# Single-bank PSUM tiles, VectorE alone for two-operand work, and the leaky gate in one ScalarE instruction, in the Strassen part of an attention and two-layer feed-forward kernel

## The chip, the core and the metric

The kernel runs on one core of one Trainium2 chip. The metric is device time in microseconds. TensorE (PE in the profile) multiplies matrices into PSUM, which has 8 banks of 512 fp32 columns in each of 128 partitions; VectorE (DVE), ScalarE (ACT) and GpSimd (POOL) do the element-wise work; SyncE (SP) issues the DMAs. In this kernel GpSimd touches SBUF tiles only.

## What is computed

A windowed attention makes a matrix `x` of 3072 tokens by 512, and two feed-forward layers follow. Cut to what matters:

```python
x = moe(attention(q, k, v, mem_k, mem_v))      # layer 1: h = x @ w_in; g = h * clip(h + 3, 0, 6) / 6; g @ w_out
h = x @ w_in2                                  # layer 2, first product: 512 -> 2048
g = np.maximum(0.01 * h, h)                    # the leaky gate
out = g @ w_out2                               # layer 2, second product: 2048 -> 512
```

The precision of fp32 is kept by writing an operand as a high part (rounded to fp32r by a copy) and a low part (the operand minus its high part), and by three products in place of one: high by high, low by high, high by low.

## The kernel before

**Blocks.** The tokens are taken in six blocks of 512 columns, features on the partitions. A matmul is 128 by 128 by 512 columns. Layer 1 (`hidden`, `output`) makes for each of 16 slices `f` of the hidden 2048 features 12 matmuls of the first product, the gate, and 12 matmuls of the second product into four PSUM banks that stay open over all 16 slices.

**The Strassen part.** The first product of layer 2 is made for two blocks at a time (three phases, p = 0, 1, 2) by a Strassen scheme: a phase has 8 steps `i`, and a step makes seven products (`seven`, in the order 1, 6, 5, 7, then 2, 3, 4) of 6 matmuls each for two slices of hidden features of both blocks. Four PSUM banks b1, b2, b3, b5 take them: products 1, 6, 5 and 7 open b1, b2, b3 and b5, and their results are read out into an SBUF tile `ut`; products 2, 3 and 4 are then accumulated on top of b1, b3 and b5. So product 2 must wait until product 1's result has been read from b1, 3 until 5's has been read from b3, and 4 until 7's has been read from b5. In code order each product is three groups of two matmuls.

The results: for the first block of the pair (slices f1 and f2) the gate's output goes to `r` and is parted into the tile `g` (`two_parts`: a copy for the high part, a subtraction for the low part); for the second block it goes to `ys` and by DMA to the DRAM array `later`, and comes back (`again`) when that block's second product is made. Between the products of a step stand two slices (12 matmuls each) of the first block's second product (`output("2", 2p, f)`, called y below): one between product 7 and product 2, one after product 4. After the 8 steps come the last slices of the first block (13, 14, 15) and 15 of the 16 slices of the second block; the sixteenth stands inside the next phase's first step.

**Operands of a phase and a step.** `x_pair` makes, around the end of the phase before, the seven right-hand operands in two quarters (`x_quarter`): four loads from `spill`, four differences (`t_1`, `sub`) and seven partings (`parts_of`). `w_set` makes the left-hand operands one step ahead: two loads into `wm`, four sums or differences of 256 columns (`form`, L830) into `st`, and four partings (`two`).

**PSUM.** Two tiles `ya` and `yb` of two banks each, two tiles `h` of one bank, one tile `at` of two banks (attention, then a Strassen bank pair). `banks_of` hands a set of four banks to a phase or a block: either `h`, `h` and the two halves of `at`, or the halves of `ya` and `yb`. Phases 0 and 2 use the first set, phase 1 the second; the blocks' second products use the set that is free. Waits are put in by the tile framework, by tile: an instruction that writes a part of a tile waits for reads of that tile that stand earlier in the program, whichever half they read.

**What sets the order.** `schedule` runs the tasks in a simulated time with a cost per task, keys as priorities and a list of engines that may take each task (the first is preferred, the second taken if the first would be much later). All products are chained, so PE's order is fixed. Differences and low parts in the Strassen part name VectorE and GpSimd; high parts name ScalarE and VectorE. Each engine then works its own list strictly in that order.

**Names of lines in the trace of before.** L877 the Strassen matmuls, L684 the second products, L630 the first product of layer 1; L281 copies and high parts; L284 differences and low parts; L894 `plus` (sums from PSUM or SBUF); L905 `leak` (the gate on SBUF); L925 and L927 the gate of product 2 (a scaled copy on ScalarE, a maximum on VectorE); L715 and L717 copies of finished outputs.

Of the kernel before, what the change touches and what calls it, by code (L numbers as in the profile page):

```python
# [35 lines left out]
N = 512  # L36
# [169 lines left out]
def tile_attn_moe_moe2(ctx: ExitStack, tc: tile.TileContext, raw, w1i, w1o, w2i, w2o, out):  # L206
# [16 lines left out]
    for y in "ab":  # L223
        pools[f"y{y}"] = (ps_y, [128, 2, 512], F32)
# [439 lines left out]
    def output(lay, j, f, c0, n):
# [8 lines left out]
        ys = list(dict.fromkeys(b for b, _ in banks))  # L673
# [31 lines left out]
    def y_out(lay, j, f, t0, n, d, y, k, two):  # L705
# [16 lines left out]
        if two and f == KF - 1:  # L722
            l = add(lambda e: nc.sync.dma_start(out=make(s), in_=half[j, d]), {"SP": dma(n * 512)}, key - 8, after=[yhalf[j, d], *firsts], allocs=[s])
            k = add(plus, {"DVE": dve(n)}, key, after=[k, l], uses=[s, y[0]])
        else:
            k = add(take, {"DVE": dve(n)} if d % 2 else {"ACT": act(n, 50.0)}, key, after=[k], allocs=[s], uses=[y[0]])
# [22 lines left out]
    def x_quarter(p, j, key, need):  # L749
# [13 lines left out]
        def sub(out, x, y, after, allocs=(), uses=()):  # L763
            return add(lambda e: minus(e, out(), x(), y()), {"DVE": dve(N), "POOL": pool(N)}, key, after=after, allocs=allocs, uses=uses)

        def parts_of(name, of, own, after):
            bufs = xop[p, name]
            first = xtask[p, name][0][:1], xtask[p, name][1][:1]
            hi = add(lambda e: copy(e, operand(p, name, 0, j).bitcast(F32R), of()), {"ACT": act(N), "DVE": dve2(N)}, key, after=after + first[0], allocs=[] if first[0] else bufs[:1], uses=[own] + (bufs[:1] if first[0] else []))
            new = not first[1] and len(bufs) == 2  # L770
            lo = add(lambda e: minus(e, operand(p, name, 1, j).bitcast(F32R), of(), operand(p, name, 0, j).bitcast(F32)), {"POOL": pool(N), "DVE": dve(N)}, key, after=[hi] + first[1], allocs=bufs[1:] if new else [], uses=[own, bufs[0]] + ([] if new else bufs[1:]))
# [21 lines left out]
        t1 = add(t_1, {"DVE": dve(N), "POOL": pool(N)}, key, after=[got["b11"], got["b12"]], allocs=[tt], uses=[src["b11"], src["b12"]])  # L793
# [12 lines left out]
    def w_set(p, i, key):  # L806
# [19 lines left out]
        def form(out, x, y, op, after, allocs=(), uses=()):  # L826
# [4 lines left out]
            return add(fn, {"DVE": dve(256), "POOL": pool(256)}, key, after=after, allocs=allocs, uses=[*raws, *uses])  # L831
# [6 lines left out]
        def two(t, src, n, after):  # L838
# [8 lines left out]
            hi = add(fn_hi, {"ACT": act(n), "DVE": dve2(n)}, key + 0.5, after=after + gate, allocs=[ts[t]], uses=[src])  # L847
            lo = add(fn_lo, {"POOL": pool(n), "DVE": dve(n)}, key + 0.6, after=[hi], uses=[src, ts[t]])
# [7 lines left out]
    def seven(p, i, n):  # L856
# [14 lines left out]
        alloc = [to[0]] if fresh and n != 7 and not (n == 6 and to[1] is not None) else []  # L871
# [11 lines left out]
        us = [to[0], t, *xb]  # L883
# [6 lines left out]
        def plus(out, x, y, opts, after, allocs=(), uses=()):  # L890
            def fn(e):
                for q in allocs:
                    make(q, ([128, 2, N], F32) if q is ut else None)
                engine(e).tensor_tensor(out=out(), in0=x(), in1=y(), op=ALU.add)  # L894
            return add(fn, opts, key, after=after, allocs=allocs, uses=uses)

        def take(q, b, after, allocs=()):
            def fn(e):
                for x in allocs:
                    make(x, ([128, 2, N], F32))  # L900
                copy(e, ut.t[:, q], bank(b))
            return add(fn, {"ACT": act(N, 50.0), "DVE": dve(N)}, key, after=after, allocs=allocs, uses=[b[0]] + ([] if allocs else [ut]))
# [154 lines left out]
```

## Time and profile before

| | |
|---|---|
| median of 3 runs | 1195.41 us (1194.85 to 1195.47) |
| the profiled execution's own time | 1192.55 us |
| its span, first to last instruction | 1190.8 us |
| PE busy | 1111.6 us, 93% of the span |
| DVE, ACT, POOL busy | 53%, 40%, 33% |
| mean granted TensorE clock | 0.987 |
| matmuls in the chain that ended last | 83% of the span |

The chain that ended last is followed back from the last instruction, and is mostly PE. So the reading asks where PE stands still: the list of waits names for each engine who ended them, the timeline shows them one by one, and the starts in the chain give the length of a step to compare with its matmuls. The first 620 us are attention and layer 1; the Strassen part runs from 627.7 us to the end.

### The profile page before, as it was taken

Reading aid. Unit: us, or ns where it says so; the run is one execution under the profiler, and the core shown is the slowest. Engines: PE = TensorE matmul, PEld = TensorE weight load, DVE = VectorE, ACT = ScalarE, POOL = GpSimd, SP = SyncE. Lnnn points to the kernel's source line nnn. Section 1 sums busy time; section 2 is a strip of 40 time slices with the busy share of each in tenths; the row PEclk is TensorE's granted clock in tenths of the full one; section 3 lists DMA queues with packets and bytes.
Section 4 is the critical chain, followed back from the end, with each engine's and each line's share of the span. In section 5 each row is a group of like instructions: output and inputs, shape, how many; then the busy total and the mean of one; then the engine's idle time right before and its main releaser. Section 6 shows DMA issues by size and latency. Waiting matters only on the chain.

```text
span 1190.8 us, 19604 instructions
## 1 busy us (share of the span) xinstructions
PE 1111.6 (93%) x7632; PEld 897.2 (75%) x7632; DVE 625.4 (53%) x988; ACT 472.5 (40%) x1154; POOL 387.7 (33%) x319
## 2 busy tenths in 40 slices
PE   4599999999999999999999999899888899999998
PEld 3487888888888888888887777677666677777776
DVE  5789975554435535415517666744544571655310
ACT  4557655445554544433324333333222332322222
POOL 1030000011232232125524443664344474444343
PEclk9699999999999999999999999899999999999999
DMA  8894454654445534321103332622121260311150
GB/s 195 256 244 143 144 152 131 180 158 134 139 140 149 138 96 131 97 62 53 36 1 115 98 104 101 209 82 80 62 62 54 74 235 19 99 61 62 38 184 36
DMA packets 85341, 135.50 MB, mean 114 GB/s; under 512 B 8448, under 2 KB 41216, under 8 KB 85248
## 3 DMA queue, kind: packets, MB, share of 16 engines
q1 hardware_dynamic: 85248, 134.25, 37.3%
q8 instruction: 60, 0.98, 0.4%
q14 instruction: 33, 0.27, 0.1%
HBM read 98.57 MB, written 35.65 MB: 113 GB/s over the span
## 4 chain that ended last, share of the span: by engine, by line
PE 83%; DVE 5%; ACT 3%; DMA 3%; issue 3%; POOL 2%; SPq 2%; POOLq 0%; DVEq 0%; ACTq 0%
PE h L630 21%; PE ya L684 15%; PE yb L684 15%; PE at L877 7%; PE h L877 5%; PE h L684 5%; PE at L684 5%; PE yb L877 4%; PE ya L877 3%; ACT w L281 2%; PE at L506 1%; DMA w<-in_w1i 1%; DMA w<-in_raw 1%; PE at L445 1%; DVE ys L894 1%
## 5 line engine op out<-in xcount | busy, mean ns | idle before, releaser
L284 POOL TENSOR_TENSOR g<-r,g 128x512 fp32r<-128x512 f32 x108 | 143.2, 1326 | 463.3 <-ACT g L281 459.2
L684 PE MATMUL ya<-g,w 128*128 128x512 f32 x864 | 266.8, 394 | 4.8 <-ACT g L281 2.1
L684 PE MATMUL yb<-g,w 128*128 128x512 f32 x864 | 264.2, 391 | 0.0
L630 PE MATMUL h<-xh,w 128*128 128x512 f32 x768 | 195.5, 395 | 1.9 <-ACT xh L281 1.9
L684 PEld LDWEIGHTS ya<-g,w 128*128 128x128 f32 x864 | 160.8, 188 | 41.0 <-ACT g L281 3.5
L684 PEld LDWEIGHTS yb<-g,w 128*128 128x128 f32 x864 | 163.1, 189 | 34.8
L630 PEld LDWEIGHTS h<-xh,w 128*128 128x128 f32 x768 | 144.2, 190 | 33.1 <-ACT xh L281 3.1
L646 DVE SCALAR_TENSOR_TENSOR r<-r,h 128x512 f32<-128x512 f32 x96 | 65.9, 686 | 171.7 <-ACT r L643 171.6
L281 ACT CAST g<-r 128x512 fp32r<-128x512 f32 x144 | 89.7, 623 | 158.2 <-DVE r L646 51.4
L643 ACT ACTIVATE r<-h,three 128x512 f32<-128x512 f32 x96 | 66.6, 693 | 155.6 <-PE h L630 155.1
L630 PE MATMUL h<-xl,w 128*128 128x512 f32 x384 | 104.4, 394 | 0.6 <-issue 0.6
L684 PE MATMUL h<-g,w 128*128 128x512 f32 x288 | 89.8, 396 | 1.5 <-DVE g L284 1.0
L684 PE MATMUL at<-g,w 128*128 128x512 f32 x288 | 89.1, 394 | 0.0
L877 PE MATMUL at<-w 128*128 128x512 f32 x288 | 74.9, 398 | 14.9 <-DVE ys L894 9.4
L630 PEld LDWEIGHTS h<-xl,w 128*128 128x128 f32 x384 | 72.2, 189 | 16.2 <-issue 1.0
L284 POOL TENSOR_TENSOR g<-w,g 128x512 fp32r<-128x512 f32 x45 | 60.3, 1340 | 55.3 <-ACT g L281 55.3
L877 PEld LDWEIGHTS at<-w 128*128 128x128 f32 x288 | 52.5, 188 | 33.1 <-DVE ys L894 14.5
L684 PEld LDWEIGHTS h<-g,w 128*128 128x128 f32 x288 | 54.8, 191 | 14.6 <-DVE g L284 1.5
L281 ACT CAST g<-w 128x512 fp32r<-128x512 f32 x48 | 29.8, 621 | 85.9 <-PE at L684 55.8
L684 PEld LDWEIGHTS at<-g,w 128*128 128x128 f32 x288 | 54.9, 191 | 11.9
L284 DVE TENSOR_TENSOR w<-st,w 128x512 fp32r<-128x512 f32 x28 | 35.9, 1294 | 48.7 <-ACT w L281 48.7
L284 POOL TENSOR_TENSOR w<-wm,w 128x512 fp32r<-128x512 f32 (+1 forms) x44 | 54.8, 1250 | 8.6 <-ACT w L281 6.7
(163 smaller groups left out, 1502.0 us busy)
## 6 DMA issues: line engine op xcount, KB each, us to landing
wm<-w322i SPq DMA_DIRECT2D x48, 256.0 KB
later<-ys SPq DMA_DIRECT2D x48, 256.0 KB
w<-later SPq DMA_DIRECT2D x24, 512.0 KB
a<-in_raw SPq DMA_DIRECT2D x44, 224.0 KB
w<-in_w1i SPq DMA_DIRECT2D x16, 512.0 KB
w<-in_w1o SPq DMA_DIRECT2D x16, 512.0 KB
w<-in_w2i SPq DMA_DIRECT2D x16, 512.0 KB
w<-in_w2o SPq DMA_DIRECT2D x16, 512.0 KB
```

Source lines behind the costliest of these rows:

```text
L281: nc.scalar.copy(out, in_) if e == "ACT" else engine(e).tensor_copy(out=out, in_=in_)
L284: engine(e).tensor_tensor(out=out, in0=a, in1=b, op=ALU.subtract)
L445: nc.tensor.matmul(ps.t[h * CHUNK:(h + 1) * CHUNK, par, i * W:(i + 1) * W], qk[h // 2].t[r, gp, (h % 2) * G + c * CHUNK:(h % 2) * G + (c + ...
L506: nc.tensor.matmul(pv.t[(h % 2) * D:(h % 2 + 1) * D, par, (h // 2) * 2 * G + i * CHUNK:(h // 2) * 2 * G + (i + 1) * CHUNK], v[h // 2].t[r, ...
L630: nc.tensor.matmul(h.t[:, :n], w.t[:, 1 if p == 1 else 0, k * 128:(k + 1) * 128], x[:, k, c0:c0 + n], start=(p == 0 and k == 0), stop=(p = ...
L643: nc.scalar.activation(out=make(r)[:, :n], in_=h.t[:, :n], func=AF.Relu, bias=three[:, 0:1], scale=1.0)
L646: nc.vector.scalar_tensor_tensor(out=r.t[:, :n], in0=r.t[:, :n], scalar=6.0, in1=h.t[:, :n], op0=ALU.min, op1=ALU.mult)
L684: nc.tensor.matmul(bank(banks[d])[:, c0:c0 + n], w.t[:, 1 if p == 1 else 0, d * 128:(d + 1) * 128], g.t[:, 1 if p == 2 else 0, :n], start= ...
L877: nc.tensor.matmul(bank(to), t.t[:, 1 if q == 1 else 0, o, kt * 128:(kt + 1) * 128], operand(p, name, 1 if q == 2 else 0, kt).bitcast(F32R ...
L894: engine(e).tensor_tensor(out=out(), in0=x(), in1=y(), op=ALU.add)
```

## The change

It edits five things, in the Strassen part and in the PSUM tiles.

1. **PSUM.** `ya`, `yb` become four one-bank tiles `y`; `at` is kept for attention and is then replaced by two one-bank tiles `hx`. The first four units of attention use two-bank tiles `ab`, `ac`, closed when the first `y` is made. A bank is now a tile, so `seven` and `output` name single tiles.
2. **Engines.** Every difference, sum and low part of `x_quarter`, `w_set`, `seven` and `again` names VectorE alone; the high parts in `x_quarter` and `w_set` name ScalarE alone. Layer 1 keeps GpSimd for its low parts.
3. **The leaky gate.** `leak` and the two instructions for product 2 become one ScalarE activation, Prelu with slope 0.01.
4. **Product 5.** It is no longer copied to `ut`; VectorE adds it to the sum of 1 and 6 at once.
5. **Product 7.** Its bank is added to that sum straight into `ys`; the extra sum over SBUF (on GpSimd or VectorE) is gone.

```diff
-    for y in "ab":
-        pools[f"y{y}"] = (ps_y, [128, 2, 512], F32)
+    for a in "bc":
+        pools[f"a{a}"] = (ps_b, [128, 2, 512], F32)
...
-    places |= {"ya": 1, "yb": 1, "h": 2, "at": 1}
+    places |= {"ab": 1, "ac": 1, "y": 4, "h": 2, "at": 1, "hx": 2}
...
+        if b.tag in ("hx", "y") and b.tag not in pools:
+
+            (attention if b.tag == "hx" else begin).close()
+            pools[b.tag] = (ctx.enter_context(tc.tile_pool(name=b.tag, bufs=places[b.tag], space=PSUM, side="right" if b.tag == "hx" else "left")), [128, 512], F32)
...
     def banks_of(other):
-        if other:
-            t = Buf("at")
-            return [(Buf("h"), None), (Buf("h"), None), (t, 0), (t, 1)]
-        a, b = Buf("ya"), Buf("yb")
-        return [(a, 0), (a, 1), (b, 0), (b, 1)]
+        return [Buf(t) for t in (("h", "h", "hx", "hx") if other else "yyyy")]
...
         def sub(out, x, y, after, allocs=(), uses=()):
-            return add(lambda e: minus(e, out(), x(), y()), {"DVE": dve(N), "POOL": pool(N)}, key, after=after, allocs=allocs, uses=uses)
+            return add(lambda e: minus(e, out(), x(), y()), {"DVE": dve(N)}, key, after=after, allocs=allocs, uses=uses)
...
-            return add(fn, {"DVE": dve(256), "POOL": pool(256)}, key, after=after, allocs=allocs, uses=[*raws, *uses])
+            return add(fn, {"DVE": dve(256)}, key, after=after, allocs=allocs, uses=[*raws, *uses])
...
-            hi = add(fn_hi, {"ACT": act(n), "DVE": dve2(n)}, key + 0.5, after=after + gate, allocs=[ts[t]], uses=[src])
-            lo = add(fn_lo, {"POOL": pool(n), "DVE": dve(n)}, key + 0.6, after=[hi], uses=[src, ts[t]])
+            hi = add(fn_hi, {"ACT": act(n)}, key + 0.5, after=after + gate, allocs=[ts[t]], uses=[src])
+            lo = add(fn_lo, {"DVE": dve(n)}, key + 0.6, after=[hi], uses=[src, ts[t]])
...
         def leak(r, after):
-            return add(lambda e: nc.vector.scalar_tensor_tensor(out=r.t, in0=r.t, scalar=0.01, in1=r.t, op0=ALU.mult, op1=ALU.max), {"DVE": dve(N)}, key, after=[after], uses=[r])
+            return add(lambda e: nc.scalar.activation(out=r.t, in_=r.t, func=AF.Prelu, alpha=0.01), {"ACT": act(N)}, key, after=[after], uses=[r])
...
-        low = {"POOL": pool(N), "DVE": dve(N)}
-        dv = {"DVE": dve(N)}
+        low = {"DVE": dve(N)}
...
         elif n == 5:
-            done[5] = take(1, b3, [k, done[1]])
+            done[5] = plus(lambda: ut.t[:, 1], lambda: bank(b3), lambda: ut.t[:, 0], [k, done[6]], uses=[ut, b3])
         elif n == 7:
-            done[7] = plus(lambda: ut.t[:, 1], lambda: bank(b5), lambda: ut.t[:, 1], dv, [k, done[5]], uses=[ut, b5[0]])
             r = Buf("ys")
-            q = plus(lambda: r.t, lambda: ut.t[:, 0], lambda: ut.t[:, 1], {"POOL": pool(N), **dv}, [done[7], done[6]], allocs=[r], uses=[ut])
-            put(r, f2, leak(r, q))
+            done[7] = plus(lambda: r.t, lambda: bank(b5), lambda: ut.t[:, 1], [k, done[5]], allocs=[r], uses=[ut, b5])
+            put(r, f2, leak(r, done[7]))
         elif n == 2:
             r = Buf("r")
-            q = add(lambda e: nc.scalar.mul(make(r), bank(b1), 0.01), {"ACT": act(N, 50.0)}, key, after=[k, *rs[-1:]], allocs=[r], uses=[b1[0]])
+            q = add(lambda e: nc.scalar.activation(out=make(r), in_=bank(b1), func=AF.Prelu, alpha=0.01), {"ACT": act(N, 50.0)}, key, after=[k, *rs[-1:]], allocs=[r], uses=[b1])
             rs.append(q)
-            q = add(lambda e: nc.vector.tensor_tensor(out=r.t, in0=bank(b1), in1=r.t, op=ALU.max), dv, key, after=[q], uses=[r, b1[0]])
             two_parts("2", a, f1, r, q, key, low)
...
-        two_parts("2", 2 * p + 1, f, r, k, key, {"POOL": pool(N), "DVE": dve(N)}, f % 2)
+        two_parts("2", 2 * p + 1, f, r, k, key, {"DVE": dve(N)}, f % 2)
```

PE's matmuls and transposes stand in the same order in both programs; what changes on PE is where it waits. First PE, in a step in the middle of phase 0, products 1, 6, 5 and 7 (`h` holds b1 and b2; `at`, later `hx`, holds b3 and b5); before:

```order
L877 MATMUL h<-xh,w 128x512 x2
L877 MATMUL h<-xh,w 128x512 [waits Pool_49]
L877 MATMUL h<-xh,w 128x512 x3
L877 MATMUL h<-xl,w 128x512 x2
L877 MATMUL h<-xl,w 128x512 [waits Pool_49]
L877 MATMUL h<-xl,w 128x512 x3
L877 MATMUL at<-w 128x512 [waits DVE_49]
L877 MATMUL at<-w 128x512 x7
L877 MATMUL at<-w 128x512 [waits Activation_49]
L877 MATMUL at<-w 128x512 x3
```

The same four products of the change, on PE:

```order
L877 MATMUL h<-xh,w 128x512 [waits Activation_49]
L877 MATMUL h<-xh,w 128x512 x5
L877 MATMUL h<-xl,w 128x512 [waits Activation_49]
L877 MATMUL h<-xl,w 128x512 x5
L877 MATMUL hx<-w 128x512 [waits DVE_49]
L877 MATMUL hx<-w 128x512 x5
L877 MATMUL hx<-w 128x512 [waits DVE_49]
L877 MATMUL hx<-w 128x512 x5
```

The wait in the middle of product 7 (the ninth matmul on `at`) is gone, and with it those in the middle of 1 and 6; every wait now stands at a product's start.

VectorE in one step of phase 0 (numbers tell buffers apart; L894 sums, L905 and L927 gate, L830 `form`, L284 low parts); before:

```order
L894 TENSOR_TENSOR w_7029<-h_7026,w_7029 128x512
L830 TENSOR_TENSOR st_7039<-wm_6985,st_7035 128x256
L284 TENSOR_TENSOR w_7059<-st_7039,w_7059 128x512
L894 TENSOR_TENSOR w_7029<-at_7043,w_7029 128x512
L905 SCALAR_TENSOR_TENSOR ys_7081<-ys_7081 128x512
L284 TENSOR_TENSOR w_7093<-wm_7061,w_7093 128x512
L927 TENSOR_TENSOR r_7100<-h_7016,r_7100 128x512
L284 TENSOR_TENSOR w_7104<-wm_7067,w_7104 128x512
L894 TENSOR_TENSOR ys_7118<-at_7043,w_7029 128x512
L905 SCALAR_TENSOR_TENSOR ys_7118<-ys_7118 128x512
L894 TENSOR_TENSOR r_7130<-at_7043,w_7029 128x512
L905 SCALAR_TENSOR_TENSOR r_7130<-r_7130 128x512
```

The same step of the change on VectorE, from product 6's sum on (L290 is what L284 was):

```order
L894 TENSOR_TENSOR w_7051<-h_7048,w_7051 128x512
L894 TENSOR_TENSOR w_7051<-hx_7057,w_7051 128x512
L830 TENSOR_TENSOR st_7075<-wm_7036 128x256
L830 TENSOR_TENSOR st_7079<-wm_7028,wm_7036 128x256
L830 TENSOR_TENSOR st_7075<-st_7075,wm_7028 128x256
L290 TENSOR_TENSOR w_7065<-wm_7028,w_7065 128x512
L830 TENSOR_TENSOR st_7079<-wm_7028,st_7075 128x256
L290 TENSOR_TENSOR w_7073<-wm_7036,w_7073 128x256
L290 TENSOR_TENSOR w_7087<-st_7075,w_7087 128x512
L290 TENSOR_TENSOR w_7095<-st_7079,w_7095 128x512
L894 TENSOR_TENSOR ys_7109<-hx_7067,w_7051 128x512
L290 TENSOR_TENSOR g_7125<-r_7118,g_7125 128x512
```

The gate's four instructions are gone from VectorE, and all four forms and four low parts of the next step's weights now stand between the sums of products 5 and 7 (rows one, two and eleven; row twelve is the low part of a `g`); after the last row the sums of products 3 and 4, two low parts of `w_out` slices and a second low part of `g` complete the step.

Last, VectorE at the change from phase 0 to phase 1, from product 3's sum in the last step on (the operands of phase 1 are made here: `a`, `xh`, `xl` and `w`); before:

```order
L894 TENSOR_TENSOR ys<-at,w 128x512
L284 TENSOR_TENSOR a<-a,w 128x512
L905 SCALAR_TENSOR_TENSOR ys<-ys 128x512
L894 TENSOR_TENSOR r<-at,w 128x512
L284 TENSOR_TENSOR xl<-w,xl 128x512
L905 SCALAR_TENSOR_TENSOR r<-r 128x512
L830 TENSOR_TENSOR st<-wm 128x256 x2
L830 TENSOR_TENSOR st<-st,wm 128x256
```

The same place on VectorE in the change:

```order
L894 TENSOR_TENSOR ys<-hx,w 128x512
L290 TENSOR_TENSOR g<-r,g 128x512
L894 TENSOR_TENSOR r<-hx,w 128x512
L290 TENSOR_TENSOR w<-a,w 128x512
L290 TENSOR_TENSOR a<-a,w 128x512
L290 TENSOR_TENSOR xl<-w,xl 128x512
L290 TENSOR_TENSOR xl<-a,xl 128x512
L290 TENSOR_TENSOR w<-a,w 128x512
L290 TENSOR_TENSOR g<-r,g 128x512
```

Both low parts of `g` (for slices 14 and 15 of block 0) and the low parts of the operands have come over from GpSimd's list, and five instructions now stand between product 4's sum (`r<-hx`) and the low part of slice 15.

## Rows read from the trace of the kernel before

**Rows 1.** The page, part 1: busy time, share of the span, instructions.

```profile
PE 1111.6 (93%) x7632; PEld 897.2 (75%) x7632; DVE 625.4 (53%) x988; ACT 472.5 (40%) x1154; POOL 387.7 (33%) x319
```

**Rows 2.** Stretch table of phase 1's steps: length, PE, PEld, DVE, ACT, POOL, clock, DMA.

```profile
813.10:942.10 129.00, 113.61 (x475) 87.16 (x474) 62.42 (x101) 32.47 (x59) 50.04 (x40) 1.00 0.23 74
```

**Rows 3.** PE's waits: who waited for whom, total us, times, longest.

```profile
PE at L877 <- ACT w L281: 10.9, 16, 0.8
PE at L877 <- DVE ys L894: 9.4, 12, 0.8
PE yb L877 <- DVE ys L894: 6.7, 7, 2.0
PE yb L877 <- ACT w L281: 5.4, 8, 0.7
PE ya L877 <- ACT w L281: 5.3, 7, 0.8
```

**Rows 4.** The chain that ended last: start, us, what.

```profile
595.04 2.72 PE h L630 x12
...
627.68 2.72 PE h L877 x12
...
813.07 2.72 PE ya L877 x12
...
844.29 1.83 PE ya L877 x8
...
862.39 1.83 PE ya L877 x8
...
1004.44 2.72 PE h L877 x12
```

**Rows 5.** Timeline, all engines, products 6, 5, 7: start, us, engine, line, what, [idle before].

```profile
709.22 1.52 PE L877 MATMUL h<-xl,w 128*128 128x512 f32 x6
709.42 0.59 ACT L281 COPY w<-h 128x512 f32<-128x512 f32 x1 [0.69 <-PE h L877]
...
712.60 0.59 ACT L281 COPY w<-at 128x512 f32<-128x512 f32 x1 [0.71 <-PE at L877]
...
713.23 0.97 PE L877 MATMUL at<-w 128*128 128x512 f32 x3 [0.68 <-ACT w L281]
```

**Rows 6.** Timeline, all engines, change from phase 0 to 1.

```profile
751.86 1.73 POOL L284 TENSOR_TENSOR w<-a,w 128x512 fp32r<-128x512 f32 x1
...
752.37 1.77 DVE L284 TENSOR_TENSOR w<-a 128x512 f32<-128x512 f32 x1
...
754.79 0.69 DVE L284 TENSOR_TENSOR a<-a 128x512 f32<-128x512 f32 x1
754.87 1.76 POOL L284 TENSOR_TENSOR xh<-w,xh 128x512 fp32r<-128x512 f32 x1 [1.28 <-ACT xh L281]
...
755.39 0.69 DVE L927 TENSOR_TENSOR r<-h,r 128x512 f32<-128x512 f32 x1
...
763.13 0.73 PE L684 MATMUL ya<-g,w 128*128 128x512 f32 x2 [1.77 <-ACT g L281]
...
764.94 2.07 PE L684 MATMUL ya<-g,w 128*128 128x512 f32 x4 [1.07 <-POOL g L284]
...
766.37 0.41 DVE L284 TENSOR_TENSOR w<-wm,w 128x256 fp32r<-128x256 f32 x1
```

**Rows 7.** Stretch table just after that wait, columns as in rows 2.

```profile
765.00:770.00 5.00, 5.00 (x12) 3.93 (x13) 4.73 (x9) 2.59 (x5) 1.33 (x1) 0.50 0.57 196
```

**Rows 8.** Timeline of ACT late in layer 1, where phase 0's operands are made.

```profile
591.35 0.62 ACT L281 CAST g<-r 128x512 fp32r<-128x512 f32 x1 [4.07 <-DVE r L646]
```

**Rows 9.** Timeline, all engines, the last matmuls and the last copies out.

```profile
1184.34 1.52 PE L684 MATMUL at<-g,w 128*128 128x512 f32 x6
...
1185.89 0.69 DVE L717 TENSOR_SCALAR ys<-at 128x512 f32<-128x512 f32 x1 [0.67 <-PE at L684]
1186.62 0.60 ACT L715 ACTIVATE ys<-at 128x512 f32<-128x512 f32 x1 [2.17 <-DVE ys L717]
```

More of the change, by code (lines that the diff above doesn't have):

```diff
@@ L672, in output @@
         banks = ybuf[lay, j]
-        ys = list(dict.fromkeys(b for b, _ in banks))
+        ys = banks
         g, w = gbuf[lay, j, f, c0], wbuf[lay + "o", f]
@@ L723, in y_out @@
             l = add(lambda e: nc.sync.dma_start(out=make(s), in_=half[j, d]), {"SP": dma(n * 512)}, key - 8, after=[yhalf[j, d], *firsts], allocs=[s])
-            k = add(plus, {"DVE": dve(n)}, key, after=[k, l], uses=[s, y[0]])
+            k = add(plus, {"DVE": dve(n)}, key, after=[k, l], uses=[s, y])
         else:
-            k = add(take, {"DVE": dve(n)} if d % 2 else {"ACT": act(n, 50.0)}, key, after=[k], allocs=[s], uses=[y[0]])
+            k = add(take, {"DVE": dve(n)} if d % 2 else {"ACT": act(n, 50.0)}, key, after=[k], allocs=[s], uses=[y])
         k = add(lambda e: nc.sync.dma_start(out=dst, in_=s.t[:, :n]), {"SP": dma(n * 512)}, key, after=[k], uses=[s])
@@ L768, in parts_of @@
             first = xtask[p, name][0][:1], xtask[p, name][1][:1]
-            hi = add(lambda e: copy(e, operand(p, name, 0, j).bitcast(F32R), of()), {"ACT": act(N), "DVE": dve2(N)}, key, after=after + first[0], allocs=[] if first[0] else bufs[:1], uses=[own] + (bufs[:1] if first[0] else []))
+            hi = add(lambda e: copy(e, operand(p, name, 0, j).bitcast(F32R), of()), {"ACT": act(N)}, key, after=after + first[0], allocs=[] if first[0] else bufs[:1], uses=[own] + (bufs[:1] if first[0] else []))
             new = not first[1] and len(bufs) == 2
-            lo = add(lambda e: minus(e, operand(p, name, 1, j).bitcast(F32R), of(), operand(p, name, 0, j).bitcast(F32)), {"POOL": pool(N), "DVE": dve(N)}, key, after=[hi] + first[1], allocs=bufs[1:] if new else [], uses=[own, bufs[0]] + ([] if new else bufs[1:]))
+            lo = add(lambda e: minus(e, operand(p, name, 1, j).bitcast(F32R), of(), operand(p, name, 0, j).bitcast(F32)), {"DVE": dve(N)}, key, after=[hi] + first[1], allocs=bufs[1:] if new else [], uses=[own, bufs[0]] + ([] if new else bufs[1:]))
             xtask[p, name][0].append(hi)
@@ L792, in x_quarter @@
         d11 = parts_of("b11", at("b11"), src["b11"], [got["b11"]])
-        t1 = add(t_1, {"DVE": dve(N), "POOL": pool(N)}, key, after=[got["b11"], got["b12"]], allocs=[tt], uses=[src["b11"], src["b12"]])
+        t1 = add(t_1, {"DVE": dve(N)}, key, after=[got["b11"], got["b12"]], allocs=[tt], uses=[src["b11"], src["b12"]])
         t2 = sub(t_at(1), at("b22"), t_at(0), [t1, got["b22"]], uses=[tt, src["b22"]])
@@ L870, in seven @@
         xb, (xhi, xlo) = xop[p, name], xtask[p, name]
-        alloc = [to[0]] if fresh and n != 7 and not (n == 6 and to[1] is not None) else []
+        alloc = [to] if fresh else []
         need = [done[{2: 1, 3: 5, 4: 7}[n]]] if n in THEN else []
@@ L888, in seven, with plus @@
         pk[p, i, n] = k
-        def plus(out, x, y, opts, after, allocs=(), uses=()):
+        def plus(out, x, y, after, allocs=(), uses=()):
             def fn(e):
                 for q in allocs:
[L893 to L902, printed above, removed]
+                    make(q)
+                nc.vector.tensor_tensor(out=out(), in0=x(), in1=y(), op=ALU.add)
+            return add(fn, {"DVE": dve(N)}, key, after=after, allocs=allocs, uses=uses)
@@ L911, in seven, with take @@
-        dv = {"DVE": dve(N)}
+        low = {"DVE": dve(N)}
         if n == 1:
-            done[1] = take(0, b1, [k], allocs=[ut])
+            def take(e):
+                make(ut, ([128, 2, N], F32))
+                copy(e, ut.t[:, 0], bank(b1))
+            done[1] = add(take, {"ACT": act(N, 50.0)}, key, after=[k], allocs=[ut], uses=[b1])
         elif n == 6:
-            done[6] = plus(lambda: ut.t[:, 0], lambda: bank(b2), lambda: ut.t[:, 0], dv, [k, done[1]], uses=[ut, b2[0]])
+            done[6] = plus(lambda: ut.t[:, 0], lambda: bank(b2), lambda: ut.t[:, 0], [k, done[1]], uses=[ut, b2])
@@ L930, in seven @@
             r = Buf("ys")
[L931 removed]
+            q = plus(lambda: r.t, lambda: bank(b3), lambda: ut.t[:, 0], [k, done[6]], allocs=[r], uses=[ut, b3])
             put(r, f1, leak(r, q))
```

17 lines of the change are left out of this document (8 added, 9 removed).

## The prediction, made before the change was run

> **What bounds the kernel now.** I read the page first: PE is busy for 93% of the span [rows 1] and the chain that ended last is mostly matmuls, so only time in which PE stands still, or runs slowly, can be won. The stretch table then says where: in the steps of phase 1, PE is busy for 113.61 of 129.00 us at a granted clock of 1.00, while VectorE is busy for less than half [rows 2]. So PE waits there, and no other engine is full.
>
> The list of PE's waits says for what: five rows of the Strassen matmuls, 16 + 12 + 7 + 8 + 7 = 50 waits, nearly all of 0.7 to 0.8 us, 37.7 us in sum, ended by a copy on ScalarE or a sum on VectorE [rows 3]. The timeline shows one of them closely [rows 5]. Product 6 runs on one `h` tile while ScalarE copies product 1 out of the other `h` tile (from 709.42 us, 0.59 us), and PE does not stop. Three microseconds later ScalarE copies product 5 out of one half of `at` (712.60 us, 0.59 us), and PE, which is in the middle of product 7 in the other half, stands still for 0.68 us until that copy is over. Nothing in product 7 needs it: tiles of one bank go on, a tile of two banks stops.
>
> The chain gives what a wait costs in all. Twelve matmuls without a wait take 2.72 us, 0.2267 us each [rows 4]. A whole step has 42 + 24 = 66 matmuls, 14.96 us. In phase 1 the same matmuls of two steps start at 844.29 and 862.39 us: 18.10 us, 3.14 us more, for the three waits of such a step. So one wait costs 3.14 / 3 = 1.05 us, more than its idle 0.68 to 0.78, since matmuls before and after it overlap less.
>
> The whole loss can be counted the same way. Phase 0 lasts from 627.68 to 813.07 us, phase 1 to 1004.44, and phase 2 to the last matmul's end, 1184.34 + 6 x 0.2267 = 1185.70 us [rows 4, 9]. They hold 720, 720 and 732 matmuls (336 of a phase's products, and 384, 384 and 396 of second products). The loss is 185.39 - 163.2 = 22.2, 191.37 - 163.2 = 28.2 and 181.26 - 165.9 = 15.3 us: 65.7 us. The 50 waits make 50 x 1.047 = 52.3 us of it. The other 13.4 us lie at the two changes of phase, where operands are made while second products run: there PE waits for the two parts of a `g` (1.77 and 1.07 us), and after them the granted clock is 0.50, the lower of its two levels (1.2 GHz), for 5 us, which costs 2.5 us more [rows 6, 7].
>
> **The change, part by part.**
>
> *Single-bank tiles.* The waits in mid-product go, as the order shows, and the price before is 52.3 us. What comes next is the wait at a product's start, for the bank that it continues. Product 3 needs product 5's sum, 4 needs 7's. The tight one is 7's, since VectorE's list now has the next step's weights between the sums of 5 and 7. From the end of product 5: its sum 0.69, four forms and a half low part 5 x 0.41, three low parts 3 x 0.69, the sum of 7 again 0.69: 5.5 us [rows 6]. PE reaches product 4 after 6 + 12 + 6 + 6 = 30 matmuls, 6.8 us. There are 1.3 us to spare, and back to back these instructions start every 0.60 us (754.79, 755.39), which adds more. So I take 0 for a new wait there; the most that it could be is what the old one was.
>
> The Trainium skill (PSUM — Partial Sum Buffer, section PSUM bank collisions raise a hardware error) asks that PSUM be guarded by bank and quadrant, so a read of one bank need not hold a matmul into another. Rows 5 agree. By that rule 52.3 us are to be had; were the pair of banks the unit, none.
>
> *VectorE in place of GpSimd.* Per step VectorE has five sums, three and a half low parts of weights, four forms, two low parts of `g`, and in phase 0 two more of `w_out`: 12 x 0.69 + 5 x 0.41 = 10.3 us of 14.96. That fits, if 0.69 is the price. Before, the same kind of instruction takes 1.77 us when a GpSimd one (1.73 us) runs beside it, and 0.69 when it does not; one that reads a PSUM bank takes 0.69 even with GpSimd at work (755.39 within 754.87 to 756.63) [rows 6]. After the change GpSimd has nothing to do in the phases. The bounds are thus 0.60 and 1.77; I take 0.69.
>
> The Trainium skill (SBUF — State Buffer, section Who interferes with whom) says that a VectorE instruction with two SBUF inputs and a GpSimd one that reads SBUF exclude each other for a whole instruction. The rows agree. By it a step costs VectorE 10.3 us; if 1.77 were its own price, 23.3, which is a rival below.
>
> *The changes of phase.* Here all that GpSimd did lands on VectorE, in order. Let product 4 of the last step end at T. Behind its sum stand five instructions of operands and then the low part of slice 15 of `g`. At T the sum of 3 and the low part of 14 may still be ahead: 2 x 0.60, then product 4's own sum 0.60, five more 3.0 and the low part 0.69: T + 5.5. PE wants it after slices 13 and 14 and two matmuls, 26 x 0.2267: T + 5.9. So it just fits, with 0.4 us. Slice 0 of the next block has seven more VectorE instructions ahead (5 x 0.41 + 2 x 0.69 = 3.4 us): its low part ends at T + 9.6 and is wanted at T + 8.16 + 8 x 0.2267 = T + 9.97. In the second quarter up to five instructions (3.0 us) stand between two low parts that PE wants 2.72 us apart, and the margin from a `g` tile's release to its need is 2.72 + 1.81 us, of which its own copy and low part take about 1.3. I expect small waits and no fall of the clock as before, and keep 2.0 of the 13.4 us. Bounds: 0, and 13.4 if nothing improves. Phase 0's own operands are made while layer 1 runs and GpSimd still works; there ScalarE once stood 4.07 us for VectorE before the copy for `g` [rows 8], and the list of PE's waits has none at that place, so I add 0.
>
> *The gate on ScalarE.* Three more instructions of 0.60 us per step and one of 0.59 fewer [rows 5, 9]: 1.2 us on an engine that is busy for 32.47 of 129.00 us [rows 2]. Hidden. VectorE loses four of 0.69. The program has one table load in both versions, at its start. Products 5 and 7 save a copy and a sum over SBUF, off PE's path.
>
> *SP's queue* has the same DMAs in slightly another order; the puts to `later` now wait for ScalarE. Hidden by a step.
>
> *The end.* The last two copies out read halves of one `at` tile, and ScalarE's starts only after VectorE's (1186.62 after 1185.89 + 0.69) [rows 9]. With a tile each, the last copy ends at about 1186.58, not 1187.22: 0.6 us.
>
> **Sum.** 52.3 + (13.4 - 2.0) + 0.6 = 64.3 us. The profiled execution, 1192.55 us, becomes 1128.3. The median of the runs shown is 2.86 us above it; taken over as it is, 1195.41 - 64.3 = 1131.1 us.
>
> **The rivals.**
>
> *The changes of phase get worse.* VectorE alone is late, PE waits, the clock falls as at 765 us. For it: some 28 instructions in about 16 us there, no slack if each takes 0.69. Against: the need of PE allows for about that. Keeping all 13.4 us gives 1195.41 - 52.9 = 1142.5; twice that, 1155.9.
>
> *The waits stay.* If another shared tile or the read of the bank itself holds PE, the steps keep 18.10 us and only the rest is won: 1195.41 - 12.0 = 1183.4. Against: `h` in rows 5, and the order.
>
> *VectorE becomes the bound, slower than before.* If its instructions cost what 752.37 shows, a step takes 12 x 1.77 + 2.05 = 23.3 us in phase 0 and 10 x 1.77 + 2.05 = 19.8 in the others, against 17.06, 18.10 and 17.06 now (14.96 and two, three, two waits): 8 x (6.2 + 1.7 + 2.7) = 85 us more, 1280. It decides from a mean of 46.1 / 32 = 1.44 us on. Against: 1.77 is seen only beside GpSimd.
>
> **How the numbers follow.** Forecast 0.85, at 1131.1. Worse changes of phase 0.10, waits that stay 0.02, VectorE the bound 0.03. Low end: no loss left is 1195.41 - 66.3 = 1129.1; if the 2.86 us between execution and median go as well, 1126.2. High end: 13.4 us kept, 1142.5. The range 1126 to 1143 holds the forecast and part of the first rival. Differences under 0.2%, about 2.4 us, a measurement cannot tell from none. Faster 0.96, same 0.01, slower 0.03.
>
> **What would show it.** Right: PE's waits without the five rows of rows 3; steps of 14.96 us in all phases; VectorE's two-SBUF instructions at 0.69 or less after 628 us; GpSimd idle from there. Changes of phase: waits of PE on `g`, and the clock after them. Wrong: steps above 15.2 us, a new wait at the start of product 4 on VectorE, or VectorE near full in the steps.

## The result, and the profile after

The changed kernel takes 1124.72 us (median of 4 runs, 1123.48 to 1126.59), against 1195.13 us for the kernel before (1190.85 to 1195.47): a ratio of 0.942, 95% interval 0.9395 to 0.9445. That is 70 us less; 64 were forecast, and the time lies 1.3 us below the range's low end. The profiled execution took 1124.98 us.

The page, busy time as in [rows 1]:

```profile
PE 1089.0 (97%) x7632; PEld 898.4 (80%) x7632; DVE 613.8 (55%) x1086; ACT 510.4 (45%) x1216; POOL 111.3 (10%) x111
```

The chain that ended last, from the first Strassen matmul on, as in [rows 4]:

```profile
627.22 2.72 PE h L877 x12
...
654.42 2.72 PE h L877 x12
...
669.38 2.72 PE h L877 x12
...
684.34 2.72 PE h L877 x12
...
741.46 8.16 PE y L684 x36
...
817.62 5.44 PE y L877 x24
...
832.58 5.44 PE y L877 x24
...
847.54 5.44 PE y L877 x24
...
912.82 40.80 PE y L684 x180
```

Steps of phase 0 start 14.96 us apart, and so do those of phase 1 (817.62, 832.58, 847.54): 66 matmuls of 0.2267 us and nothing else. The list of PE's waits has no row of the Strassen part left, neither those of [rows 3] nor one on a `g`. The timeline, all engines, over products 5 and 7, as in [rows 5]:

```profile
716.82 2.88 PE L877 MATMUL hx<-w 128*128 128x512 f32 x12
717.09 0.69 DVE L894 TENSOR_TENSOR w<-h,w 128x512 f32<-128x512 f32 x1 [1.39 <-ACT w L287]
718.38 0.69 DVE L894 TENSOR_TENSOR w<-hx,w 128x512 f32<-128x512 f32 x1 [0.60 <-PE hx L877]
718.99 0.75 DVE L830 TENSOR_TENSOR st<-wm 128x256 f32<-128x256 f32 x2
```

VectorE reads product 5 from one `hx` at 718.38 while PE runs product 7 into the other: twelve matmuls in one piece, where PE had stood 0.68 us in the middle of product 7.

VectorE and PE at the change from phase 0 to 1, where [rows 6] had waits of 1.77 and 1.07 us:

```profile
740.75 0.68 DVE L290 TENSOR_TENSOR g<-r,g 128x512 fp32r<-128x512 f32 x1
...
741.30 6.05 PE L684 MATMUL y<-g,w 128*128 128x512 f32 x26
...
741.50 0.69 DVE L894 TENSOR_TENSOR r<-hx,w 128x512 f32<-128x512 f32 x1
...
742.11 0.69 DVE L290 TENSOR_TENSOR w<-a,w 128x512 fp32r<-128x512 f32 x1
...
745.12 0.69 DVE L290 TENSOR_TENSOR g<-r,g 128x512 fp32r<-128x512 f32 x1
```

And the stretch table behind it, as [rows 2] and [rows 7]:

```profile
747.00:802.00 55.00, 55.00 (x244) 45.57 (x243) 29.93 (x53) 20.40 (x36) 0.00 (x0) 1.00 0.33 110
```

PE is busy for all 55.00 us at a granted clock of 1.00; GpSimd is idle. The last matmuls and copies out, as [rows 9]:

```profile
1118.02 1.52 PE L684 MATMUL hx<-g,w 128*128 128x512 f32 x6
...
1118.90 0.60 ACT L715 ACTIVATE ys<-hx 128x512 f32<-128x512 f32 x1 [0.76 <-PE hx L684]
1119.58 0.69 DVE L717 TENSOR_SCALAR ys<-hx 128x512 f32<-128x512 f32 x1 [0.67 <-PE hx L684]
```

Each bank is copied out as soon as it is done. From the start of the last matmuls to the span's end (1123.2) pass 5.2 us, where 6.5 passed before (1184.34 to 1190.8).

### The profile page after: what moved, and what is told of

Its sections match the earlier page's. It is cut to its first block, busy times and chain, and to the rows that moved or that the text cites. A ratio compares the mean times of both kernels' runs of the same rounds, so it can differ in the third digit from the quotient of the medians.

```text
span 1123.2 us, 19440 instructions
## 1 busy us (share of the span) xinstructions
PE 1089.0 (97%) x7632; PEld 898.4 (80%) x7632; DVE 613.8 (55%) x1086; ACT 510.4 (45%) x1216; POOL 111.3 (10%) x111
## 4 chain that ended last, share of the span: by engine, by line
PE 90%; DMA 5%; DVE 2%; SPq 1%; ACT 1%; issue 1%; DVEq 0%; ACTq 0%
PE y L684 33%; PE h L636 22%; PE hx L877 8%; PE y L877 7%; PE hx L684 6%; PE h L684 6%; PE h L877 6%; DMA w<-in_raw 2%; DMA w<-in_w1i 1%; PE at L512 1%; PE at L451 1%; DMA w<-in_w1o 1%; SPq L416 1%; PE at L501 1%; DVE w L290 0%
## 5 line engine op out<-in xcount | busy, mean ns | idle before, releaser
L684 PE MATMUL y<-g,w 128*128 128x512 f32 x1728 | 416.8, 390 | 0.0
L684 PEld LDWEIGHTS y<-g,w 128*128 128x128 f32 x1728 | 323.2, 188 | 67.6
L290 POOL TENSOR_TENSOR g<-r,g 128x512 fp32r<-128x512 f32 x64 | 88.1, 1376 | 324.9 <-ACT g L287 320.2
L290 DVE TENSOR_TENSOR g<-r,g 128x512 fp32r<-128x512 f32 x80 | 56.8, 710 | 95.0 <-ACT g L287 95.0
L684 PE MATMUL hx<-g,w 128*128 128x512 f32 x288 | 87.7, 389 | 0.0
L290 DVE TENSOR_TENSOR g<-w,g 128x512 fp32r<-128x512 f32 x48 | 33.2, 691 | 70.8 <-ACT g L287 70.8
L877 PE MATMUL hx<-w 128*128 128x512 f32 x288 | 69.2, 389 | 0.0
L684 PEld LDWEIGHTS hx<-g,w 128*128 128x128 f32 x288 | 54.1, 188 | 11.2
L877 PEld LDWEIGHTS hx<-w 128*128 128x128 f32 x288 | 54.1, 188 | 11.2
L290 DVE TENSOR_TENSOR w<-wm,w 128x512 fp32r<-128x512 f32 x88 | 54.5, 621 | 12.8 <-ACT w L287 12.7
L287 ACT CAST w<-wm 128x512 fp32r<-128x512 f32 x88 | 48.6, 561 | 12.3 <-DVE wm L355 11.1
```

Of the source, the lines that this page charges most:

```text
L287: nc.scalar.copy(out, in_) if e == "ACT" else engine(e).tensor_copy(out=out, in_=in_)
L290: engine(e).tensor_tensor(out=out, in0=a, in1=b, op=ALU.subtract)
L684: nc.tensor.matmul(bank(banks[d])[:, c0:c0 + n], w.t[:, 1 if p == 1 else 0, d * 128:(d + 1) * 128], g.t[:, 1 if p == 2 else 0, :n], start= ...
L877: nc.tensor.matmul(bank(to), t.t[:, 1 if q == 1 else 0, o, kt * 128:(kt + 1) * 128], operand(p, name, 1 if q == 2 else 0, kt).bitcast(F32R ...
```

## The experiments

Every trace holds the same work up to the first Strassen matmul, which starts between 625.24 and 629.76 us in the thirteen traces read (627.52 before, 627.06 after). So I compare, beside medians, the **Strassen part**: the profiled execution's time minus that start. It is 565.03 us before and 497.92 after, 67.1 less. Each ratio is against runs of before on the same chip. I also count from the order of each program the **false waits**: matmuls in the middle of a product that wait until ScalarE or VectorE has read another part of their PSUM tile. The last column tells where PE loses time: how much longer than 0.2267 us per matmul the steps take, from the first Strassen matmul of a phase to its last, and in the same way the stretches behind the steps (the changes of phase, and the end of phase 2).

| kernel | median, us | ratio, 95% interval | false waits in the program, in the trace | Strassen part, us | lost in the steps, behind them, us |
|---|---|---|---|---|---|
| before | | | 50, 50 | 565.03 | 52.9, 13.0 |
| after | 1124.72 | 0.942 (0.9395–0.9445) | 0, 0 | 497.92 | 0, 0 |
| e1, banks alone | 1142.35 | 0.9567 (0.9543–0.9591) | 0, 0 | 515.23 | 0, 17.3 |
| e2, engines, gate, products 5 and 7 | 1154.24 | 0.967 (0.9654–0.9686) | 26, 26 | 527.20 | 27.8, 0.1 |
| e7, engines alone | 1179.41 | 0.9898 (0.9877–0.9918) | 51, 51 | 551.83 | 52.6, 0.1 |
| e8, gate, products 5 and 7 alone | 1196.87 | 1.004 (1.0026–1.0053) | 55, 55 | 569.24 | 66.3, 3.8 |
| e3, after with GpSimd back | 1135.28 | 0.9511 (0.9492–0.9529) | 0, 0 | 508.63 | 0, 10.7 |
| e4, after with the old gate | 1127.32 | 0.944 (0.9416–0.9464) | 0, 0 | 498.07 | 0, 0 |
| e6, after with GpSimd beside | 1148.49 | 0.9633 (0.9616–0.9649) | 0, 0 | 519.28 | 10.4, 11.0 |
| e5, after, 14 more on VectorE | 1129.65 | 0.9463 (0.9448–0.9478) | 0, 0 | 501.88 | 2.9, 0.3 |
| e5b, after, 28 more on VectorE | 1249.48 | 1.0483 (1.0466–1.0501) | 0, 0 | 621.51 | 115.7, 7.9 |

### Each half alone

The single-bank tiles alone (the edit of the tile pools left out):

```diff
...
-        if other:
-            t = Buf("at")
-            return [(Buf("h"), None), (Buf("h"), None), (t, 0), (t, 1)]
-        a, b = Buf("ya"), Buf("yb")
-        return [(a, 0), (a, 1), (b, 0), (b, 1)]
+        return [(Buf(t), None) for t in (("h", "h", "hx", "hx") if other else "yyyy")]
```

> The kernel before with nothing changed but the PSUM tiles (one bank each); GpSimd, the gate and products 5 and 7 as before. Theory (the mid-product waits come from two banks sharing a tile): all 50 waits of PE in the Strassen products go, steps take 14.96 us in every phase, the two changes of phase keep most of their 13.4 us: 52 to 55 us less than before, about 1141. Rival (the waits were the slow readers, GpSimd and a contended VectorE): less than 30 us, and waits of PE on VectorE stay.

They win 49.8 us of the Strassen part, the steps lose nothing any more, and the tail is that of after: the theory held. The median is 51.9 us below before's, just under the 52 to 55 expected, for the changes of phase did not keep their 13.0 us but lose 17.3. All engines there, and the stretch table from the same place on:

```profile
744.91 1.79 DVE L907 SCALAR_TENSOR_TENSOR ys<-ys 128x512 f32<-128x512 f32 x1
...
746.11 1.74 POOL L290 TENSOR_TENSOR g<-r,g 128x512 fp32r<-128x512 f32 x1
...
750.87 0.74 PE L686 MATMUL y<-g,w 128*128 128x512 f32 x2 [1.77 <-ACT g L287]
```

```profile
750.00:755.00 5.00, 3.07 (x8) 2.14 (x9) 5.00 (x8) 2.03 (x4) 2.71 (x3) 0.69 0.36 110
755.00:760.00 5.00, 5.00 (x16) 3.94 (x15) 3.36 (x5) 1.98 (x4) 3.16 (x3) 0.63 0.74 264
```

VectorE and GpSimd hold each other (1.79 and 1.74 us), PE waits 1.77 us for `g`, and right after that the granted clock is 0.69 and 0.63 on the mean of these stretches. The other half alone keeps the two-bank tiles:

```diff
-            return add(fn, {"DVE": dve(256), "POOL": pool(256)}, key, ...)
+            return add(fn, {"DVE": dve(256)}, key, ...)
...
-            done[5] = take(1, b3, [k, done[1]])
+            done[5] = plus(lambda: ut.t[:, 1], lambda: bank(b3), lambda: ut.t[:, 0], dv, [k, done[6]], uses=[ut, b3[0]])
```

> The kernel before with the PSUM tiles kept at two banks; VectorE alone for two-operand work, the gate as one ScalarE activation, products 5 and 7 shortened. Theory: the mid-product waits stay (two per step in phases 0 and 2, three in phase 1), only the 13.4 us at the changes of phase go: 10 to 15 us less than before, about 1182. Rival (freeing VectorE shortens the waits): 30 us less or more.

My theory missed: 37.8 us of the Strassen part are gone, not 10 to 15, though the tiles still have two banks. PE's waits in it:

```profile
PE at L877 <- DVE ys L894: 7.1, 9, 0.8
PE at L877 <- DVE w L894: 6.3, 8, 0.8
PE ya L877 <- ACT w L281: 4.7, 7, 0.7
```

With two single waits on `yb`, 26 are left of 50. The rival's number came (30 us or more), but not for its reason: the waits are fewer and not shorter, at up to 0.8 us each. PE and VectorE of this kernel, first in phase 0, then in phase 2:

```profile
660.96 0.69 DVE L894 TENSOR_TENSOR w<-at,w 128x512 f32<-128x512 f32 x1 [1.05 <-PE at L877]
...
661.70 1.21 PE L877 MATMUL at<-w 128*128 128x512 f32 x4 [0.79 <-DVE w L894]
```

```profile
1009.12 1.52 PE L877 MATMUL at<-xl,w 128*128 128x512 f32 x6
1010.15 0.42 DVE L284 TENSOR_TENSOR w<-wm,w 128x256 fp32r<-128x256 f32 x1
...
1010.48 0.62 PE L684 MATMUL ya<-g,w 128*128 128x512 f32 x2
1010.68 0.69 DVE L894 TENSOR_TENSOR w<-at,w 128x512 f32<-128x512 f32 x1
```

In phase 2 the sum of product 5 starts when product 7 is over. VectorE's list has the low parts of the next weights ahead of it, so in the program the sum stands behind product 7's matmuls, and these have no read to wait for. A false wait is thus a matter of program order too. If so, the waits counted from the program should price any such kernel. The next two split e2's edit:

> Before, with the two-bank tiles, the old gate and the old products 5 and 7; only the lists of engines change (VectorE alone for two-operand work, ScalarE alone for high parts). Theory: the time is counted from the waits that the program holds. In before the program has 50 waits of a matmul in mid-product on ScalarE or VectorE, and the trace showed 50; with both halves of the edit but the old tiles it has 26, and the trace showed 26. This kernel has 51 by the order of its program (14, 22 and 15 in the three phases), since product 5 is still copied by ScalarE at once, so they cost 51 x 1.05 = 53 us; the 13 to 17 us at the changes of phase go, as GpSimd is out of them. So 1124.7 + 53.4 + 1.4 (tail) = about 1179 us, 15 below before, and no wait of the second products on g. Rival: VectorE alone is what won the 40 us of the two together, then 1155 to 1160.

> Before, with the two-bank tiles and GpSimd; only the leaky gate as one ScalarE activation and the shorter products 5 and 7. Theory: the order of the program has 55 waits in mid-product on ScalarE or VectorE (16, 23 and 16), 5 more than before, 5 us; the loss at the changes of phase stays or falls by a microsecond or two with four fewer VectorE instructions per step: 1194 to 1200 us, the same as before or a little slower. Rival: the shorter products 5 and 7 take the copy out of mid-product by themselves and win 25 us or more: 1170 or less.

e7's edit is the first piece of e2's diff, for all two-operand work; e8's is the second piece with product 7's shorter sum, and Prelu. Both times came out as expected, at 1179.41 and 1196.87 us, e8's by luck, as is told below. PE's waits in e7, then the first two rows of e8's:

```profile
PE at L877 <- ACT w L281: 10.8, 16, 0.7
PE at L877 <- DVE ys L894: 10.4, 13, 1.0
...
PE yb L877 <- DVE ys L894: 5.7, 7, 1.0
PE yb L877 <- ACT w L281: 5.4, 8, 0.7
PE ya L877 <- ACT w L281: 4.7, 7, 0.7
```

```profile
PE at L877 <- DVE w L894: 16.2, 16, 1.3
PE at L877 <- DVE ys L894: 13.9, 16, 2.2
```

In e7 51, and none on `g`. Beside after, with 1.3 us for the tail, a false wait costs (551.83 - 497.92 - 1.3) / 51 = 1.03 us in e7 and (527.20 - 497.92 - 1.3) / 26 = 1.08 in e2, around the 1.05 of the prediction. In e8 they are dearer: 55 have 49.5 us of idle time, 0.90 each, where before's 50 have 37.7, 0.75. In all a wait costs 1.20 us in e8's steps (66.3 / 55) and 1.06 in before's (52.9 / 50). That e8's time still came out is luck: its steps lose 13.4 us more than before's, where five more waits at 1.05 were expected, and the stretches behind them 9.2 less (3.8 for 13.0), where one or two were. e8 has no wait on a `g` either, though GpSimd works as before.

So e7 wins 13.2 us, e8 loses 4.2, and together they win 37.8. By the counts (51, 55 and 26) the read of product 5 moves behind product 7 only when VectorE does it and VectorE's list is long; that is read from the programs, and no further run tries it.

### GpSimd beside VectorE

After, with the old lists of engines:

```diff
...
-        low = {"DVE": dve(N)}
+        low = {"POOL": pool(N), "DVE": dve(N)}
...
```

> The changed kernel with GpSimd allowed again wherever it was before (differences, forms, low parts). Theory: steps hold 14.96 us, GpSimd works beside VectorE again, VectorE instructions of 1.77 us come back, and PE waits for parts of g at the changes of phase: 5 to 13 us more than the changed kernel. Rival (the gate and product 5 and 7 alone made room enough): within 2 us of the changed kernel.

10.7 us more, as expected. All engines at the change from phase 0 to 1:

```profile
748.19 1.71 POOL L290 TENSOR_TENSOR g<-r,g 128x512 fp32r<-128x512 f32 x1
748.70 1.75 DVE L290 TENSOR_TENSOR xh<-a,xh 128x512 fp32r<-128x512 f32 x1
...
749.95 2.50 PE L684 MATMUL y<-g,w 128*128 128x512 f32 x5 [1.44 <-POOL g L290]
```

From 750 to 755 us the granted clock is 0.50, and PE makes 12 matmuls where 22 fit at 0.2267 us. e6 leaves every list of the other engines as it is and gives GpSimd work that nobody reads:

```diff
...
         pk[p, i, n] = k
+        for _ in range(2):
+            add(lambda e: minus(e, spare, spare, spare), {"POOL": pool(256)}, key, after=[k])
```

> The changed kernel with two more GpSimd subtractions of 128 x 256 on a scratch tile after each product, 14 per step, which nobody reads (0.74 us each in the trace of before). The lists of all other engines stay as they are. Theory: GpSimd beside VectorE is what made VectorE's instructions with two SBUF inputs last 1.77 us. Of some 17 VectorE instructions in a step about 11 have two SBUF inputs, and each that meets one of GpSimd's is held for 0.3 to 1.1 us, so VectorE needs 13.6 to 22 us per step instead of 10.3; PE waits again, at the changes of phase first: 3 to 40 us more than the changed kernel, and rows of VectorE well above 0.69 us in the steps. Rival: the 1.77 us came from something else, such as the operands' transfers: no row above 0.75 us in the steps, and the time of the changed kernel within 2 us.

The theory held in phase 0: 21.4 us more in the Strassen part, 10.4 of them in the steps of phase 0, which take some 16.7 us, and 11.0 at the change to phase 1. But the added work does not come 14 to a step. Nothing makes GpSimd wait for a product, and its 336 subtractions run in one piece from the first step until late in phase 1; so phase 2 tests nothing. In phase 1 the steps stay at 14.96 us even beside GpSimd: there VectorE's list lacks the low parts of `w_out`. GpSimd, then VectorE beside it in phase 0:

```profile
628.54 284.70 POOL L292 TENSOR_TENSOR spare<-spare 128x256 f32<-128x256 f32 x336
...
701.71 0.68 DVE L898 TENSOR_TENSOR ys<-hx,w 128x512 f32<-128x512 f32 x1
...
711.54 1.58 DVE L832 TENSOR_TENSOR st<-wm 128x256 f32<-128x256 f32 x2
...
713.80 1.10 DVE L292 TENSOR_TENSOR w<-wm,w 128x512 fp32r<-128x512 f32 x1
```

With both inputs in SBUF, a pair of 128 x 256 takes 1.58 us where such a pair takes 0.75 in after (718.99), and one of 128 x 512 takes 1.10 for 0.69. The sum that reads a PSUM bank keeps its 0.68, although GpSimd works without a gap.

The Trainium skill (SBUF — State Buffer, section Who interferes with whom) says that a VectorE instruction with two SBUF inputs contends with a GpSimd one that reads SBUF, over ports that only one of them can hold, and that one with at most one SBUF input, outside the modes that use both ports, does not. VectorE's three rows agree.

### The gate, and VectorE's room

After with the gate of before (product 2's maximum and `leak` on VectorE):

```diff
-            return add(lambda e: nc.scalar.activation(out=r.t, in_=r.t, func=AF.Prelu, alpha=0.01), {"ACT": act(N)}, ...)
+            return add(lambda e: nc.vector.scalar_tensor_tensor(out=r.t, in0=r.t, scalar=0.01, in1=r.t, op0=ALU.mult, op1=ALU.max), {"DVE": dve(N)}, ...)
...
```

> The changed kernel with the leaky gate back on VectorE (a scaled copy on ScalarE and a maximum for product 2; one instruction over SBUF for the others). VectorE gets 4 x 0.60 = 2.4 us more per step, 11.3 of 14.96 us in phase 0. Theory: the steps hold 14.96 us, and the changes of phase, which had about 1.4 us to spare, lose 0 to 3 us: 0 to 3 us more than the changed kernel. Rival (the gate on ScalarE carries part of the gain): 8 us more or beyond.

The Strassen part is 498.07 us, 0.15 more than in after. So the place of the gate is worth nothing here, as VectorE has room. How much, e5b and e5 tell, with four and two more VectorE instructions after each product (e6's diff with `DVE`):

> The changed kernel with four more VectorE subtractions of 128 x 256 on a scratch tile after each product, 28 per step, which nobody reads. It prices the rival in which VectorE becomes the bound. Theory: back to back such instructions start every 0.34 us and those of 512 columns every 0.60 us, so VectorE needs 18.4 us per step in phase 0 and 17.2 us in the others against PE's 14.96: 8 x 3.4 + 16 x 2.2 = 63 us more, about 1188, somewhat more with what is lost at the changes of phase; PE waits at the start of products on VectorE. By the durations of single instructions (0.41 and 0.69 us) it would be 141 us more, about 1266.

It came out between the two numbers, 123.6 us more. VectorE in it:

```profile
684.90 0.69 DVE L292 TENSOR_TENSOR g<-r,g 128x512 fp32r<-128x512 f32 x1
685.50 1.80 DVE L292 TENSOR_TENSOR spare<-spare 128x256 f32<-128x256 f32 x4
687.22 0.68 DVE L898 TENSOR_TENSOR ys<-hx,w 128x512 f32<-128x512 f32 x1
```

The kernel's own instructions start 0.60 us apart; the added ones, each of which reads what the one before wrote, 0.43. With these, and 8.9 us of the kernel's own (12 x 0.60 + 5 x 0.34), VectorE needs 28 x 0.43 + 8.9 = 20.94 us per step in phase 0 and 19.74 in the others: 8 x 5.98 + 16 x 4.78 = 124 us more than PE's 14.96 (126 in the next expectation is a slip of mine). VectorE can become the bound.

> The changed kernel with two more VectorE subtractions of 128 x 256 on a scratch tile after each product, 14 per step. With 28 per step VectorE was the bound: four such instructions took 1.72 us from start to start, 0.43 each (each waits for the one before, as all write one tile), and 12 x 0.60 + 5 x 0.34 = 8.9 us of the kernel's own make 20.9 us per step in phase 0 (21.3 in the trace) and 19.7 in the others, 126 us more than the changed kernel against 124.8 measured. Theory: with half of them VectorE needs 6.0 + 8.9 = 14.9 us of 14.96 in phase 0 and 13.7 in the others, so the steps stay at 14.96 or a few tenths above in phase 0, and the changes of phase lose a few microseconds: 1125 to 1134. Rival: the margin of the single sums (1.3 us at product 4) decides, not the sum over a step: each such wait costs up to 1 us per step, 1140 to 1150.

Held: 4.0 us more in the Strassen part, most of it in phase 0, whose steps take 15.3 us. The change leaves VectorE 6 us of a step of phase 0 free.

### Where executions differ

> The changed kernel as it is, once more. In ten traces so far, whose first part is the same work, the first Strassen matmul starts between 625.2 and 628.2 us, and from there to the end the changed kernel took 497.9 us. Theory: the microseconds between one execution and another of the same kernel arise in the first 110 us, where loads set the pace and the granted clock falls to 0.5 at times; so in this trace the Strassen part takes 497.9 us again, to within 0.3, and the start accounts for the rest; median 1123.5 to 1127. Rival: the 2.9 us between the median and the profiled execution of before come from taking the profile or from the Strassen part: then the timed executions lie above the profiled one by about 2.9 us, or the Strassen part varies by more than 1 us.

> As the run before, for a third trace of the changed kernel: start of the Strassen part between 625 and 628.5 us, and 497.9 us from there to the end to within 0.3.

> The kernel before, once more, for a second trace of it: start of the Strassen part between 625 and 628.5 us, and 565.0 us from there to the end to within 1 us (1192.55 - 627.52 in the first trace); 50 waits in mid-product again.

a1's profiled execution took 5373.6 us, with all matmuls some six times as long, and gives no trace to compare; its four others took 1121.53 to 1129.88 us. a2 took 1127.67 us and b1 1191.56. PE at the first Strassen matmul, a2 then b1:

```profile
629.76 1.52 PE L877 MATMUL h<-xh,w 128*128 128x512 f32 x6
```

```profile
626.81 1.52 PE L877 MATMUL h<-xh,w 128*128 128x512 f32 x6
```

The Strassen parts are 497.91 and 564.75 us, against 497.92 and 565.03 in the first traces. So the Strassen part repeats to 0.3 us in these two pairs, and what differs between executions lies ahead of it. Most of it is there by 113 us: PE's last wait before layer 1 runs steadily, on a copy of ScalarE, is over at 108.17 us in e3 and 113.09 in a2, and the Strassen part starts 517.07 and 516.67 us later. My theory named the granted clock too, and that is borne out in part. In the 4 us behind that wait it is 0.57 to 0.62 in after, e5, e7 and e8, whose Strassen parts start 518.1 to 518.8 us after the wait; in the other nine traces it is 1.00, and they start 516.5 to 517.1 us after it. Ahead of the wait no such link shows: from 40 to 70 us the clock is 1.00 in e2, e5b, e6 and e7, which start at 626.51 to 627.60 us, and 0.68 in e3 and 0.62 in a2, which start first and last. What else sets the first 110 us stays open.

## Why the prediction was right or wrong

**The single-bank tiles: right.** 50 waits at 1.05 us were forecast to go, and no new one to come at a product's start. Both hold: before's steps lose 52.9 us and e1's none, and e7 and e2 price a wait at 1.03 and 1.08. At product 4, where 1.3 us were to spare, the sum of product 7 runs from 722.47 to 723.16 us in after's trace, and PE gets there 12 matmuls after 722.26, at 724.98: 1.8 us.

**VectorE in place of GpSimd: right, with the price too high.** The instructions take 0.69 us, the value taken; as they start 0.60 us apart, a step costs VectorE 8.9 us and not 10.3. The rival of VectorE as the bound did not come. e5 and e5b show that it exists: with some 6 us more per step phase 0 begins to lose, and with 12 every step loses 4 to 6 us.

**The changes of phase: right in kind, sized too small.** 2.0 of 13.4 us were kept, and 0 are left. I put the low part of slice 15 at T + 5.5 us; with T = 741.30 it ends at 745.81, T + 4.5, since the sum of 3 and the low part of 14 (over at 741.43), which I had queued behind T, run ahead of it; PE wants it at T + 5.9. I had credited the changes of phase to GpSimd's absence. e7, e3 and e1 bear that out: without GpSimd no wait on `g` even with the old tiles, with it 10.7 and 17.3 us lost. But it is not the only cause: e3 loses 6.6 us less than e1, and e8, which keeps GpSimd, loses 3.8 us behind its steps for before's 13.0. So the gate on ScalarE with the shorter products 5 and 7 takes off part of that loss too; which of the two does it was not tried.

**The gate: right.** Hidden on ScalarE, and e4 shows that with GpSimd out of the way it would have been on VectorE.

**The end: too small.** 0.6 us were forecast and 1.3 came. The last copy out ends 0.9 us after the last matmul (1120.27 after 1119.38), as forecast; from there to the span's end pass 2.9 us, where 3.6 passed before (1187.22 to 1190.8), which I had not looked at. Why the last puts are over sooner was not tried.

**The step that failed** is the last one, from the profiled execution to the median. The terms gave 64.3 us of 67.1: 2.0 are missing at the changes of phase and 0.7 at the end. Taken from 1192.55 us they make 1128.3, inside the range. I then added the 2.86 us by which the median of three runs lay above the profiled execution, as if every execution of the kernel had them. They are scatter: 33 timed executions of before, beside all these runs, took 1189.87 to 1196.40 us with a median of 1192.35, so 1195.41 lay near the top. Of the miss of 6.4 us, 2.8 are the terms and 3.6 this base: the 2.86 us, 0.5 by which the Strassen part starts earlier in after's trace than in before's, and 0.3 by which the median lies below the profiled execution. The low end of 1126.2 had no loss left and the 2.86 us off, and still lies 1.5 us too high: it lacks the 0.7 at the end, and it has no room for the scatter of single executions, the other 0.8. That scatter is no smaller than the gap: the four timed executions of a1, the same kernel, have a median of 1126.3, inside the range.

## What to carry to other kernels

Count the false waits in the order of the program, kernel by kernel, and multiply them by what one costs in the trace: for e7 that gave 1179 us, and it took 1179.41, closer than its executions agree (1178.29 to 1181.75). The price has to come from a kernel whose engines are as busy: in e8 a wait cost 1.20 us and not 1.05. Two edits that remove the same waits, or that remove them only together, don't add up, so measure each alone and both. And take a forecast from the part of the trace that repeats (here to 0.3 us in two pairs of traces), with the scatter of the rest in the range and not in the sum.

## What was not expected of the hardware

VectorE instructions that read what the one before wrote start further apart than others of their size: 0.43 us for the added 128 x 256 subtractions in e5b, while the second of the independent pair at 718.99 in after's trace starts 0.33 us after the first (0.75 in all, 0.42 each). The data dependence is the difference that the program shows; that it is the cause was not tried by itself. And the gate on VectorE, an instruction that reads one SBUF tile as both inputs, is held beside GpSimd like a subtraction of two tiles: 1.79 us in e1, for 0.69 in e4, where GpSimd stands still.
